# A recurrent attention and feed-forward kernel: heads of two pairs swapped over the array's rows from chunk 6 on

## The chip, the cores and the metric

One Trainium2 chip, one of its cores. The metric is device microseconds of one launch: the lower, the better. PE is the matrix engine, DVE the vector engine, ACT the scalar engine, POOL the general engine; SP only issues transfers here.

## What is computed

A linear recurrence over 768 time steps for 4 batches of 8 heads of size 48, then a feed-forward layer with a sigmoid gate:

```python
for t in range(S):
    cur = np.einsum('bhd,bhe->bhde', u[None] * kt, vt)
    y[:, :, t] = np.einsum('bhd,bhde->bhe', rt, state + cur)
    state = wt[:, :, :, None] * state + np.einsum('bhd,bhe->bhde', kt, vt)
...
h = x @ w_in                                    # x: 3072 tokens of 384, w_in: 384 x 2048
out = (h / (1 + np.exp(-1.702 * h))) @ w_out    # w_out: 2048 x 384
```

## The kernel before

**Chunks.** The 3072 tokens are 24 chunks of 128 (`chunk(t)`), six to a batch; the first chunk of a batch has no state to read, the last one makes none. Two heads are a pair, one in rows 0 to 63 of the array and one in rows 64 to 111 (`head(0)`, `head(1)`); there are four pairs. A chunk goes through these steps: two scans on DVE (lines 253, 259) give the products of decays; `kq` holds scaled keys and queries (274, 275); `ps_t` turns the keys round and ACT copies them to `kt` (309); ACT writes the eight diagonals of `am` (322); `ps_u` makes the new state (333), `sf`; `ps_s` are the scores, one bank of PSUM for each of the two row halves (351); DVE puts them into `am` where they count (354). Then the chunk's output is made of two parts on PE: `am` times the values (K is 128, two column halves) and the queries times the state (K is 64 or 48). ACT rounds the output into `x` (223) and DVE subtracts to get the remainder (224).

**Plain and crossed chunks.** Up to chunk 11 the two parts of the output go into one PSUM tile, `ps_y` (391, then 399): a head's rows and its output's partitions are the same half, so that the state part uses two of the array's four quarters. From chunk 12 on (`CROSS`) the two heads of pairs 2 and 3 are loaded with their rows swapped, in six transfers; the output is two tiles, `ps_c0` and `ps_c1` (363 for the state part, which comes first, then 369), one for each row half, and the state part uses all four quarters. Each of the two tiles is rounded and subtracted by itself. `x` of a crossed group has its blocks in another order on its lower rows.

**PSUM.** `ps_d`, `ps_t`, `ps_u`, `ps_s`, `ps_y` and `ps_c` share three buffers (`ps_a`, tag `psa`), taken in turn in the order in which the program asks for them: a tile waits until the third tile before it has been read for the last time.

**Feed-forward.** A group is four chunks. `ph` is x times a slice of w_in (two buffers), ACT makes `gh` and `gf` of it, DVE `gl`, and PE adds their products with w_out to `po`. Matmuls of 512 columns at float32r. The first 32 tasks use the whole array (lines 446 to 448 and 478 to 480), the later ones interleave the two row halves (504).

**Order.** Until task 32 the order on every engine is written out in the table `RAMP` (lN: a load of chunk N, aN: its next step, fN: a load of weights, wN: a step of their conversion, gN, hN, yN: the task N's three parts, xN: the moves that fill up x, kN: N matmuls that only keep PE busy); after that `PARTS` places the steps. Each engine works in its order, and a wait holds up all that is behind it on that engine. In `RAMP` the loads are issued by SP, later by POOL.

Of the kernel before, what the change touches and what calls it, by code (L numbers as in the profile page):

```python
# [8 lines left out]
F32 = mybir.dt.float32  # L9
# [50 lines left out]
RAMP = """  # L60
l0 l1 l0 a0 M l0 a0 a0 k20 a0 m0 m0 l1 a1 f1 l2 a0 f3 a1 l1 a0 a0 a1 k6 a0 l2 m1 a0 a1 a1 m1 a1 a0 a2 k5 a0 a1
a2 w1 k1 a1 a2 a1 k3 a2 l3 m2 f0 a2 a1 a3 a0 f0 k1 a2 k6 a1 l3 a3 l4 a2 a2 a3 a2 m3 k2 a3 a3 f6 a2 w0 a1 a4 k1
a3 w0 k6 a2 f2 l4 f8 l5 m3 a3 a3 a3 a3 a2 w1 f4 m2 k10 a3 f2 a3 a4 f8 w1 a4 w1 m4 k14 a4 a4 x3 l6 w0 w0 f11 a4
w2 a4 k3 a4 w2 a5 a4 g0 f4 h0 w2 g1 w2 g2 a5 f6 y0 w3 h1 g3 w4 w3 w4 h2 f10 f5 w3 m4 w3 y1 w4 f7 g4 y2 h3 a5 a4
y3 a5 w5 h4 w4 w6 l5 w5 m5 a5 w6 y4 g5 w5 g6 h5 f9 w6 w5 g7 w6 a5 w8 a4 a6 h6 w7 w8 w7 a6 a5 a5 a5 w8 a6 g8 a4
y5 h7 m6 f10 w8 w7 y6 h8 a5 w10 l7 g9 w7 a6 y7 h9 g10 a6 a7 m5 w10 y8 w9 w9 u a6 l6 a5 h10 a6 a5 w10 w9 a6 g11
w10 y9 g12 a7 h11 l8 w9 a7 h12 a7 w11 a7 l9 m7 a6 g13 w11 a6 g14 a7 w11 a8 w11 y10 a6 l7 h13 a6 a7 m6 a7 l8 a8
y11 m7 a8 g15 a7 l9 a7 a8 m8 a8 l10 a8 y12 h14 a7 a9 a7 a8 a9 a8 y13 a8 m8 y14 a8 a9 a9 m9 a9 l10 a9 a10 a8 m9
# [3 lines left out]
h26 y26 h27 y27 g28 g29 h28 g30 h29 a13 g31 a12 h30 y28 a12 a13 a13 m13 y29 a12 a12 h31 a13 a13 a13 m13 l14 l14  # L72
"""
WIDE = 512
CROSS = 12
WP = NF * DM // NL
SPLIT = range(FIRST, len(TASKS) - 1)
PHASE = 8
# [6 lines left out]
def rwkv_ffn_kernel(ctx: ExitStack, tc, wkr, vp, vrk, ub, w_in, w_out, masks, vt, uc, out):  # L85
# [58 lines left out]
    def load(t):  # L144

        assert t < 2 or loaded.get(t - 2, [None])[0] is None
        a, v = lands[t % 2], values[t % 3]
        loaded[t] = [a[0:R2], v]
        first, last = (TOP if t == 0 else 0), (R2 if t % (NT - 1) == 0 else P)
        rows = wkr.rearrange("t r w -> (t r) w")[t * R + first - TOP : t * R + last - TOP]  # L150
        n = NP * CW + 1
        if t < CROSS:
            for c0, c1 in ((0, n), (n, a.shape[1])) if t < 2 else ((0, a.shape[1]),):
                if c0:
                    yield
                behind_moves(queue[0].dma_start(a[first:last, c0:c1], rows[:, c0:c1]))
        else:
            w_, kr = slice(1, n), slice(n, a.shape[1])
            for cols, n_ in ((w_, 1), (kr, 2)):
                dst, src = (y[:, cols].rearrange("r (n q) -> r n q", n=n_) for y in (a, wkr[t]))  # L160
                one, two = (slice(h * dst.shape[2] // 2, (h + 1) * dst.shape[2] // 2) for h in range(2))
                queue[0].dma_start(dst[TOP:R2, :, one], src[:, :, one])
                for h in range(2):
                    rows = slice(TOP + h * D, TOP + (h + 1) * D)
                    queue[0].dma_start(dst[rows, :, two], src[(1 - h) * D : (2 - h) * D, :, two])
        yield
        assert t < 3 or t - 3 in weighed
        queue[0].dma_start(v[:, TOP:], vrk[t, :, 0:DM])
        if t >= WHOLE:
            rk = pools["late"].tile([P, 2 * DM], F32, tag="rk", name="rk_t")  # L170
            queue[0].dma_start(rk, vrk[t, :, DM:])
            loaded[t].append(rk)
        yield
# [3 lines left out]
    def fetch(i):  # L177

        s, which = divmod(i, 2)
        n = SL // NL  # L180
        st = staged[i] = wt.tile([P, n, 2 * WP // n], I32, tag=f"w{i}", name=f"raw{i}")
        src = (w_in, w_out)[which][s * n : (s + 1) * n].bitcast(I32)
        if which == 0:
            if s == 0:
                nc.sync.dma_start(st[TOP:], src[:, 0 : P - TOP].rearrange("n p w -> p n w"))
            else:
                rows = w_in.bitcast(I32).rearrange("s p w -> (s p) w")[s * n * P - TOP : (s + 1) * n * P - TOP]
                nc.sync.dma_start(st, rows.rearrange("(n p) w -> p n w", p=P))
            yield
            nc.sync.dma_start(st[0:TOP], src[:, P - TOP :].rearrange("n p w -> p n w"))  # L190
        else:
            nc.sync.dma_start(st, src.rearrange("n p w -> p n w"))
        yield

    def convert(i, pool, clamp):
# [44 lines left out]
    def chunk(t):  # L240
# [38 lines left out]
        if t < WHOLE:  # L279
            ps_d = ps_a.tile([P, NP, 2], F32, tag="psa", name="ps_d")  # L280
            for p in range(NP):
                T.matmul(ps_d[:, p], rk[:, p], u_heads[:, p], start=True, stop=True)
        yield
        if t < WHOLE:
            V.tensor_copy(s, ps_d.rearrange("p n h -> p (n h)"))
# [38 lines left out]
        def update():  # L324

            if final:
                return
            ps_u = ps_a.tile([R2, NP, D], F32, tag="psa", name="ps_u")
            for p in range(NP):

                for h in range(2):
                    c = TOP + name(p, h) * D
                    T.matmul(ps_u[head(h), p], kt[:, p, head(h)], v[:, c : c + D], start=True, stop=True)  # L333
            new = state[t] = states[t % 2]
            flat = ps_u.rearrange("r p d -> r (p d)")
# [19 lines left out]
        yield  # L355
        cs = slice(col * C, (col + 1) * C)
        if cross:
            ps = [ps_a.tile([R2, 2, C], F32, tag="psa", name=f"ps_c{r_}") for r_ in range(2)]
            each = [(p, r_, r_ ^ p // 2) for p in (0, 2, 1, 3) for r_ in range(2)]
            if sf is not None:  # L360
                for p, r_, o in each:
                    c = p * D
                    T.matmul(  # L363
                        ps[r_][head(o), p % 2], sf[head(r_), c + o * TOP : c + HB], qf[head(r_), p],
                        start=p in (0, 2), stop=False, skip_group_check=True,
                    )
            for p, r_, o in each:
                c = (2 * p + o) * D
                T.matmul(  # L369
                    ps[r_][head(o), p % 2], v[:, c + o * TOP : c + HB], am[r_][:, p],  # L370
                    start=sf is None and p in (0, 2), stop=p in (1, 3), skip_group_check=True,
                )
            weighed.add(t)
            yield
            if i not in xs:
                xs[i] = new_x(i)
            for b, y in enumerate(ps):
                split(*(xs[i][0:R2, n_, 2 * b : 2 * b + 2, cs] for n_ in range(2)), y)
# [30 lines left out]
        state.pop(t - 1, None)  # L409
        yield  # L410

    def fill_x(x, c0, c1, cross=False):

        for m in range(NM):
            for i, dst in enumerate((R2, 0)):
                j = TOP * (2 * m + i + 1)
                move = G.dma_start(  # L417
                    x[dst : dst + TOP, :, m ^ 2 * (cross and i == 0), c0:c1].bitcast(F32),
                    x[j : j + TOP, :, NM ^ 2 * (cross and j >= HB), c0:c1].bitcast(F32),
                )  # L420
                moves.append(move.ins.name)

# [14 lines left out]
    def first_product(j, task):  # L437
# [2 lines left out]
        plain = j < PLAIN  # L440
        ph = ps_h.tile([P, WIDE], F32, tag="ph", name="ph")[:, 0 : (c1 - c0) * C]
        o = by_twos(ph, plain)
        x = xs.get((i, 0), xs[i])
        for c in range(NM):
            h_, l_ = weight(0, f, c)
            T.matmul(o, h_, halves(x[:, 0, c, cs], plain), start=c == 0, stop=False)  # L446
# [66 lines left out]
    def first_rows(j, half):  # L513

        i, c0, c1, f = TASKS[j]
        cs = slice(c0 * C, c1 * C)
        if half == 0:
            parts[j] = ph_tile(c1 - c0)
        for n in range(3 * NM):
            c, term = divmod(n, 3)  # L520
            h_, l_ = weight(0, f, c)
            w, x = ((h_, 0), (h_, 1), (l_, 0))[term]
            end = n == 3 * NM - 1
            on_rows(
                half, ("h", j), parts[j], w, xs[i][:, x, c ^ 2 * (half and starts[i] >= CROSS), cs],
                half == 0 and n == 0, half == 1 and end, half == 0 and end,
            )
            yield
# [44 lines left out]
    def store(i, start, N, order=range(NM)):  # L573
# [9 lines left out]
            (A if late else queue[0]).dma_start(out[m, :, bass.ds(start, N)], ob)  # L583
        po.pop(i)
        xs.pop(i)
        xs.pop((i, 0), None)

    def new_x(i):

# [2 lines left out]
    with tc.manual_schedule():  # L592
# [17 lines left out]
        def do(token):  # L610
# [7 lines left out]
            elif kind == "x":  # L618
                group, col = where[i]
                if col == CHUNKS[group] - 1:  # L620
                    fill_x(xs[group], 0, (col + 1) * C, i >= CROSS)
            elif kind == "c":
                x = xs[i, 0] = new_x(i)
                for c in range(NM):
                    for rows, src in ((slice(0, HB), c), (slice(HB, P), c ^ 2)):
                        G.dma_start(x[rows, :, c].bitcast(F32), xs[i][rows, :, src].bitcast(F32))
            elif kind == "u":
                nc.sync.dma_start(u_sb, ub)
            elif kind == "M":
                A.dma_start(hm[TOP:R2], masks)  # L630
                for x in states + [v[:, 0:TOP] for v in values]:
                    G.memset(x, 0.0)
            elif kind == "k":
# [15 lines left out]
        def rest():  # L649
# [17 lines left out]
                        plan.setdefault(at_, []).append(token)  # L667
            for j in range(FIRST, len(TASKS) + LAG):
                for post in range(2):
                    if post and j == len(TASKS) - WHOLE:  # L670
                        yield f"c{len(CHUNKS) - 1}"
                    if post and j <= SPLIT[-1] + 1:
                        yield f"r{j}"
                        if j > SPLIT[0]:
# [137 lines left out]
```

## Time and profile before

| | us |
|---|---|
| median of 3 runs | 508.38 (506.61 to 509.78) |
| profiled execution | 508.68 |
| its span on the core | 506.7 |
| PE busy | 495.0 (98%) |
| ACT busy, DVE busy | 283.0, 285.3 (56% each) |

The table's busy times are over the whole span; the stages differ. Until about 47 us PE works mostly on matmuls that keep it busy while the first group's x is made, and from there to about 501 us it has feed-forward work in front of it all the time. DVE and ACT are nearly full until about 120 us and have room afterwards.

### The profile page before, as it was taken

To read this page: it belongs to the slowest core of one execution; us is meant where nothing else is said; L and a number is where in the kernel's file an instruction comes from. 1 tells how busy PE (TensorE), PEld (TensorE's weight loads), DVE (VectorE), ACT (ScalarE), POOL (GpSimd) and SP (SyncE) were. 2 spreads that over 40 slices of the span, in tenths; PEclk is the share of its full clock that TensorE was granted. 3 is DMA by queue.
4 is the path that set the end of the run, shared out by engine and by line. 5 is a ranking of instruction groups with operands and counts; after the bars stand their busy time and mean duration, and the time that the engine had idled before them with its cause. 6 is when DMAs were issued, how large, how long until landed. Compare 5 with 4: busy or idle time off the path is not lost.

```text
span 506.7 us, 11314 instructions
## 1 busy us (share of the span) xinstructions
PE 495.0 (98%) x4535; PEld 416.3 (82%) x4535; DVE 285.3 (56%) x443; ACT 283.0 (56%) x616; POOL 70.9 (14%) x144
## 2 busy tenths in 40 slices
PE   7999999999999999999999999999999999999995
PEld 4676788887888888888888889888888888888884
DVE  7898999998886213665565555556455421211110
ACT  4887989977865543366356365455465432422322
POOL 2002000000100200044103145104140002220000
PEclk9999999999999999999999999999999999999999
DMA  8996960125463300035112235112240001150001
GB/s 278 290 403 162 335 223 12 54 93 188 117 206 103 82 13 0 1 111 157 34 49 44 84 101 166 32 48 49 82 129 29 1 1 33 42 148 1 1 0 70
DMA packets 18171, 50.27 MB, mean 99 GB/s; under 512 B 3392, under 2 KB 7168, under 8 KB 18112
## 3 DMA queue, kind: packets, MB, share of 16 engines
q1 hardware_dynamic: 11376, 31.23, 19.0%
q0 software_dynamic: 6336, 17.72, 12.7%
q8 instruction: 38, 0.62, 0.5%
q10 hardware_dynamic: 400, 0.53, 0.3%
q14 instruction: 21, 0.17, 0.1%
HBM read 40.82 MB, written 4.72 MB: 90 GB/s over the span
## 4 chain that ended last, share of the span: by engine, by line
PE 85%; DMA 7%; DVE 3%; ACT 1%; SPq 1%; issue 0%; ACTq 0%; DVEq 0%
PE po L504 26%; PE ph L504 24%; DMA raw<-in_w_in 5%; PE po L478 4%; PE po L480 4%; PE po L479 4%; PE ph L446 4%; PE ph L448 4%; PE ph L447 4%; PE ps_s L351 3%; PE ps_c L369 2%; DMA v_t<-in_vrk 2%; PE ps_u L333 2%; PE ps_y L391 1%; PE ps_y L399 1%; PE ps_c L363 1%
## 5 line engine op out<-in xcount | busy, mean ns | idle before, releaser
L504 PE MATMUL ph<-x,pair 64*128 64x512 f32 x1134 | 185.7, 377 | 0.0
L464 DVE TENSOR_TENSOR gl<-gf,gh 128x512 fp32r<-128x512 f32 x96 | 66.3, 691 | 185.6 <-ACT gf L463 184.7
L504 PE MATMUL po<-gh,pair 64*128 64x512 f32 x768 | 157.8, 385 | 0.2 <-SPq L509 0.2
L504 PEld LDWEIGHTS ph<-x,pair 64*128 64x128 f32 x1134 | 143.6, 186 | 13.9
L463 ACT ACTIVATE gh<-ph 128x512 fp32r<-128x512 f32 x84 | 50.2, 597 | 159.1 <-PE ph L504 137.2
L504 PEld LDWEIGHTS po<-gh,pair 64*128 64x128 f32 x768 | 95.8, 187 | 10.5 <-issue 1.1
L504 PE MATMUL po<-gl,pair 64*128 64x512 f32 x384 | 99.3, 376 | 0.0
L322 ACT ACTIVATE am<-ident,s 128x128 f32<-128x128 f32 x192 | 58.7, 396 | 3.8 <-PE ps_y L391 2.3
L504 PEld LDWEIGHTS po<-gl,pair 64*128 64x128 f32 x384 | 50.1, 186 | 4.7
L417 POOL DMA_DIRECT2D x<-x x36 | 18.2, 512 | 247.7 <-DVE x L224 209.5
L463 ACT ACTIVATE gf<-ph 128x512 f32<-128x512 f32 x84 | 49.8, 593 | 0.0
L446 PE MATMUL ph<-x,pair 128*128 128x512 f32 x99 | 39.1, 395 | 1.2 <-DMA x<-x 0.6
L448 PE MATMUL ph<-x,pair 128*128 128x512 f32 x99 | 38.1, 385 | 0.2 <-DVE pair L214 0.2
L447 PE MATMUL ph<-x,pair 128*128 128x512 f32 x99 | 38.0, 384 | 0.0
L478 PE MATMUL po<-gh,pair 128*128 128x512 f32 x96 | 37.9, 394 | 0.0
L480 PE MATMUL po<-gl,pair 128*128 128x512 f32 x96 | 36.8, 384 | 0.0
L479 PE MATMUL po<-gh,pair 128*128 128x512 f32 x96 | 36.8, 383 | 0.0
L229 ACT ACTIVATE junk<-lp 112x1032 bf16<-112x1032 f32 x24 | 25.7, 1069 | 12.4 <-DVE lp L259 12.3
L253 DVE TENSOR_TENSOR_SCAN lp<-wkr_t,d1r 112x516 f32<-112x516 f32 x24 | 29.4, 1225 | 1.2 <-DMA wkr_t<-in_wkr 0.9
L259 DVE TENSOR_TENSOR_SCAN lp<-wkr_t,d1f 112x516 f32<-112x516 f32 x24 | 29.4, 1224 | 0.1
L354 DVE COPY_PREDICATED am<-after,ps_s 128x512 f32<-128x512 int32 x40 | 26.8, 724 | 1.9 <-PE ps_s L351 1.9
L229 ACT ACTIVATE junk<-kq 112x1024 bf16<-112x1024 f32 x24 | 25.4, 1058 | 1.4 <-DVE kq L275 1.3
(89 smaller groups left out, 640.4 us busy)
## 6 DMA issues: line engine op xcount, KB each, us to landing
wkr_t<-in_wkr SPq DMA_DIRECT2D x10, 770.5 KB, 5.4
raw<-in_w_out SPq DMA_DIRECT2D x6, 1024.0 KB, 11.2
raw<-in_w_in SPq DMA_DIRECT2D x5, 1024.0 KB, 11.8
rk_t<-in_vrk POOLq DMA_DIRECT2D x9, 384.0 KB, 3.6
out_t<-ob POOLq DMA_DIRECT2D x12, 256.0 KB, 2.7
v_t<-in_vrk SPq DMA_DIRECT2D x15, 192.0 KB, 4.9
rk_t<-in_vrk SPq DMA_DIRECT2D x7, 384.0 KB, 3.5
x<-x POOLq DMA_DIRECT2D x36, 64.0 KB, 2.6
```

The costliest lines, as they stand in the source:

```text
L229: A.activation(junk[:, 0 : x.shape[1]], x, AF.Square, accum_out=acc[0:R2, i : i + 1])
L253: V.tensor_tensor_scan(li.rearrange("r p c -> r (p c)")[:, ::-1], w1[:, ::-1], d1r.rearrange("r p c -> r (p c)")[:, ::-1], 0.0, op0=ALU.mu ...
L322: A.activation(x_[:, p], ident, AF.Copy, scale=s[:, j : j + 1])
L446: T.matmul(o, h_, halves(x[:, 0, c, cs], plain), start=c == 0, stop=False)
L447: T.matmul(o, h_, halves(x[:, 1, c, cs], plain), start=False, stop=False)
L448: T.matmul(o, l_, halves(x[:, 0, c, cs], plain), start=False, stop=c == NM - 1)
L463: A.activation(g, ph, AF.Gelu_apprx_sigmoid, scale=1.0 / W_SCALE)
L464: V.tensor_tensor(gl, gf, gh.bitcast(F32), op=ALU.subtract)
L478: T.matmul(o, h_, halves(gh, plain), start=first, stop=False, skip_group_check=True)
L479: T.matmul(o, l_, halves(gh, plain), start=False, stop=False, skip_group_check=True)
L480: T.matmul(o, h_, halves(gl, plain), start=False, stop=f == NF - 1, skip_group_check=True)
L504: mm = T.matmul(by_twos(out), w[rows], halves(x[rows]), start=start, stop=stop, skip_group_check=True)
```

## The change

From chunk 6 on (instead of 12) the heads of pairs 2 and 3 are swapped over the rows. The output of a crossed chunk now goes into one tile for pairs 0 and 1 and one for pairs 2 and 3, with every head on the partitions that it has in a plain chunk, so that x has one order for all groups: `fill_x` and `first_rows` lose their special cases, and the copy of the last group's x (`c`, six transfers by POOL) is gone. A crossed chunk's rows are loaded in nine transfers. A second, swapped copy of u (`um`) is loaded by POOL for chunks 6 and 7. In `RAMP` the load of chunk 6's rows (l6) stands behind most loads of weights, and loads of weights that stand behind x3 carry the wait for its moves themselves.

```diff
-a3 ... a4 a4 x3 l6 w0 w0 f11 a4
+a3 ... a4 a4 x3 w0 w0 f11 a4 w2
...
-... w5 m5 a5 w6 y4 g5 w5 g6 h5 f9 w6 w5 g7 w6 ...
+... w5 m5 a5 w6 y4 g5 w5 g6 h5 f9 l6 w6 w5 g7 w6 ...
...
-CROSS = 12
+CROSS = 6
...
+    um = cp.tile([R2, H], F32, name="um")
+    G.memset(um, 0.0)
+    u_crossed = um.rearrange("r (p h) -> r p h", h=2)
...
-            w_, kr = slice(1, n), slice(n, a.shape[1])
-            for cols, n_ in ((w_, 1), (kr, 2)):
-                ...
-                queue[0].dma_start(dst[TOP:R2, :, one], src[:, :, one])
+            for c0, n_ in ((1, n - 1), (n, NP * C), (n + NP * C, NP * C)):
+                one, two = (slice(c0 + h * n_ // 2, c0 + (h + 1) * n_ // 2) for h in range(2))
+                behind_moves(queue[0].dma_start(a[TOP:R2, one], wkr[t, :, one]))
                 for h in range(2):
                     rows = slice(TOP + h * D, TOP + (h + 1) * D)
-                    queue[0].dma_start(dst[rows, :, two], src[(1 - h) * D : (2 - h) * D, :, two])
+                    queue[0].dma_start(a[rows, two], wkr[t, (1 - h) * D : (2 - h) * D, two])
...
-            ps = [ps_a.tile([R2, 2, C], F32, tag="psa", name=f"ps_c{r_}") for r_ in range(2)]
+            ps = [ps_a.tile([R2, 2, C], F32, tag="psa", name=f"ps_c{b}") for b in range(2)]
...
-                        ps[r_][head(o), p % 2], sf[head(r_), c + o * TOP : c + HB], qf[head(r_), p],
+                        ps[p // 2][head(o), p % 2], sf[head(r_), c + o * TOP : c + HB], qf[head(r_), p],
...
-                    ps[r_][head(o), p % 2], v[:, c + o * TOP : c + HB], am[r_][:, p],
+                    ps[p // 2][head(o), p % 2], v[:, c + o * TOP : c + HB], am[r_][:, p],
...
-                    x[dst : dst + TOP, :, m ^ 2 * (cross and i == 0), c0:c1].bitcast(F32),
-                    x[j : j + TOP, :, NM ^ 2 * (cross and j >= HB), c0:c1].bitcast(F32),
+                    x[dst : dst + TOP, :, m, c0:c1].bitcast(F32),
+                    x[j : j + TOP, :, NM, c0:c1].bitcast(F32),
...
-                    if post and j == len(TASKS) - WHOLE:
-                        yield f"c{len(CHUNKS) - 1}"
```

PE, where the output of chunk 10 (`ps_y`, `ps_c`) is followed by the scores of chunk 11 (the second pair of `ps_s`); in brackets the semaphores that an instruction waits for. Before:

```order
L399 MATMUL ps_y<-kq,sf 64x128
L399 MATMUL ps_y<-kq,sf 48x128
L351 MATMUL ps_s_1763<-kq 128x128 [waits PE_49]
L351 MATMUL ps_s_1764<-kq 128x128 [waits PE_49]
L351 MATMUL ps_s_1763<-kq 128x128
L351 MATMUL ps_s_1764<-kq 128x128
```

Now:

```order
L370 MATMUL ps_c_1793<-am,v_t 48x128
L370 MATMUL ps_c_1794<-am,v_t 48x128
L370 MATMUL ps_c_1794<-am,v_t 64x128
L352 MATMUL ps_s_1832<-kq 128x128 [waits PE_49]
L352 MATMUL ps_s_1833<-kq 128x128 [waits DVE_49]
L352 MATMUL ps_s_1832<-kq 128x128
L352 MATMUL ps_s_1833<-kq 128x128
```

The third tile before `ps_s_1833` was one of chunk 10's own scores' tiles; it is now `ps_c_1793`, chunk 10's first output tile, and the wait for PE itself has become one for DVE. Between the two score tiles stands nothing else.

DVE in the same place, from chunk 10's `copy_predicated` to chunk 11's. Before:

```order
L354 COPY_PREDICATED am<-after,ps_s_1692 128x512
L259 SCALAR_TENSOR_TENSOR lp<-wkr_t,d1f 112x516
L269 TENSOR_TENSOR rk_t<-rk_t 128x384
L274 TENSOR_TENSOR kq<-wkr_t,lp 112x512
L275 SCALAR_TENSOR_TENSOR kq<-wkr_t,live,lp 112x512
L464 TENSOR_TENSOR gl<-gf,gh 128x512
L224 TENSOR_TENSOR x<-ps_y,x 112x4x128
L287 TENSOR_TENSOR rk_t<-rk_t,u_sb 128x384
L288 TENSOR_REDUCE s<-rk_t 128x8
L354 COPY_PREDICATED am<-after,ps_s_1763 128x512
```

Now:

```order
L355 COPY_PREDICATED am<-after,ps_s_1760 128x512
L260 SCALAR_TENSOR_TENSOR lp<-wkr_t,d1f 112x516
L270 TENSOR_TENSOR rk_t<-rk_t 128x384
L275 TENSOR_TENSOR kq<-wkr_t,lp 112x512
L276 SCALAR_TENSOR_TENSOR kq<-wkr_t,live,lp 112x512
L465 TENSOR_TENSOR gl<-gf,gh 128x512
L225 TENSOR_TENSOR x<-ps_c_1793,x 112x2x128
L225 TENSOR_TENSOR x<-ps_c_1794,x 112x2x128
L288 TENSOR_TENSOR rk_t<-rk_t,u_sb 128x384
L289 TENSOR_REDUCE s<-rk_t 128x8
L355 COPY_PREDICATED am<-after,ps_s_1832 128x512
```

One subtraction has become two in the same place; the one of `ps_c_1793` is the last reader of that tile. On ACT the two roundings of chunk 10 stand, as the one did, behind the eight diagonals of chunk 11.

SP, where the rows of chunk 9 stand ahead of the values of chunks 7 and 8. Before:

```order
L156 DMA wkr_t<-in_wkr 128x1541 x2
L168 DMA v_t<-in_vrk 128x384 x2
L171 DMA rk_t<-in_vrk 128x768
```

Now (the same, after the nine transfers of chunk 8):

```order
L163 DMA wkr_t<-in_wkr 96x258
L166 DMA wkr_t<-in_wkr 48x258 x2
L163 DMA wkr_t<-in_wkr 96x256
L166 DMA wkr_t<-in_wkr 48x256 x2
L163 DMA wkr_t<-in_wkr 96x256
L166 DMA wkr_t<-in_wkr 48x256 x2
L169 DMA v_t<-in_vrk 128x384 x2
L172 DMA rk_t<-in_vrk 128x768
```

SP has eight more transfers to issue ahead of the two chunks' values.

## Rows read from the trace of the kernel before

**Rows 1.** The page, part 2: PE's busy tenths in 40 slices.

```profile
PE   7999999999999999999999999999999999999995
```

**Rows 2.** Waits of PE, whole span: us in total, times, longest us.

```profile
PE ph L446 <- DMA x<-x: 0.6, 1, 0.6
...
PE ps_t L308 <- DVE kq L274: 0.5, 1, 0.5
```

**Rows 3.** Timeline of PE: chunks 9's and 10's outputs, 11's scores; start us, us.

```profile
145.08 1.09 PE L391 MATMUL ps_y<-am,v_t 128*64 128x128 f32 x16
...
156.96 1.09 PE L391 MATMUL ps_y<-am,v_t 128*64 128x128 f32 x16
157.98 1.08 PE L399 MATMUL ps_y<-kq,sf 64*64 64x128 f32 x16
159.00 1.16 PE L351 MATMUL ps_s<-kq 64*128 64x128 f32 x16
```

**Rows 4.** Timeline of PE, chunk 13 (crossed).

```profile
232.62 0.67 PE L363 MATMUL ps_c<-kq,sf 64*64 64x128 f32 x16
233.22 1.09 PE L369 MATMUL ps_c<-am,v_t 128*64 128x128 f32 x16
234.13 0.62 PE L333 MATMUL ps_u<-v_t,kt 128*48 128x48 f32 x16
```

**Rows 5.** Timeline of ACT, from chunk 10's diagonals to its rounding; idle time in brackets.

```profile
146.25 2.45 ACT L322 ACTIVATE am<-ident,s 128x128 f32<-128x128 f32 x8 [1.50 <-issue]
...
157.85 1.06 ACT L229 ACTIVATE junk<-lp 112x1032 bf16<-112x1032 f32 x1 [4.52 <-DVE lp L259]
...
159.87 2.44 ACT L322 ACTIVATE am<-ident,s 128x128 f32<-128x128 f32 x8
162.21 0.57 ACT L223 CAST x<-ps_y 112x512 fp32r<-112x512 f32 x1
```

**Rows 6.** Timeline of DVE, chunk 10.

```profile
153.37 0.69 DVE L464 TENSOR_TENSOR gl<-gf,gh 128x512 fp32r<-128x512 f32 x1 [1.18 <-ACT gf L463]
...
155.33 1.31 DVE L354 COPY_PREDICATED am<-after,ps_s 128x512 f32<-128x512 int32 x2
...
162.81 0.69 DVE L224 TENSOR_TENSOR x<-ps_y,x 112x512 fp32r<-112x512 f32 x1 [1.74 <-ACT x L223]
```

**Rows 7.** Lines 224 and 223: duration ns min/median/max, first and last start, forms.

```profile
L224 DVE TENSOR_TENSOR x<-ps_c,x x24: 413/420/427, 209.0 to 423.1; 112x256 fp32r<-112x256 f32 x24
...
L223 ACT CAST x<-ps_c x24: 372/375/378, 208.6 to 422.7; 112x256 fp32r<-112x256 f32 x24
```

**Rows 8.** Clock: timeline of PE at the start, windows at the end (PEclk after POOL).

```profile
2.82 6.07 PE L493 MATMUL idle<-d1r 112*128 112x512 bf16 x20 [2.82 <-POOL v_t L632]
...
9.96 1.46 PE L493 MATMUL idle<-d1r 112*128 112x512 bf16 x6
...
500.00:503.00 3.00, 1.21 (x6) 0.72 (x4) 0.00 (x0) 1.74 (x3) 0.00 (x0) 1.00 0.49 175
504.00:506.70 2.70, 0.00 (x0) 0.00 (x0) 0.00 (x0) 0.00 (x0) 0.00 (x0) 0.58 0.08 24
```

**Rows 9.** Weights' last early issue (SP), their landing, chunk 6's first scan (DVE).

```profile
51.57 0.37 SPq L192 DMA_DIRECT2D raw<-in_w_out  x1
...
DMA to landing us min/median/max: 7.7/11.1/18.4
...
76.81 1.23 DVE L253 TENSOR_TENSOR_SCAN lp<-wkr_t,d1r 112x516 f32<-112x516 f32 x1
```

**Rows 10.** Chunk 7's values: SP's issue, PE's use, transfers' us from issue to landing.

```profile
106.99 0.86 SPq L168 DMA_DIRECT2D v_t<-in_vrk  x2
...
113.42 0.62 PE L333 MATMUL ps_u<-v_t,kt 128*48 128x48 f32 x16
...
v_t<-in_vrk SPq DMA_DIRECT2D x15, 192.0 KB, 4.9
v_t<-in_vrk POOLq DMA_DIRECT2D x9, 192.0 KB, 2.8
```

More of the change, by code (lines that the diff above doesn't have):

```diff
@@ L62 @@
 a2 w1 k1 a1 a2 a1 k3 a2 l3 m2 f0 a2 a1 a3 a0 f0 k1 a2 k6 a1 l3 a3 l4 a2 a2 a3 a2 m3 k2 a3 a3 f6 a2 w0 a1 a4 k1
-a3 w0 k6 a2 f2 l4 f8 l5 m3 a3 a3 a3 a3 a2 w1 f4 m2 k10 a3 f2 a3 a4 f8 w1 a4 w1 m4 k14 a4 a4 x3 l6 w0 w0 f11 a4
-w2 a4 k3 a4 w2 a5 a4 g0 f4 h0 w2 g1 w2 g2 a5 f6 y0 w3 h1 g3 w4 w3 w4 h2 f10 f5 w3 m4 w3 y1 w4 f7 g4 y2 h3 a5 a4
-y3 a5 w5 h4 w4 w6 l5 w5 m5 a5 w6 y4 g5 w5 g6 h5 f9 w6 w5 g7 w6 a5 w8 a4 a6 h6 w7 w8 w7 a6 a5 a5 a5 w8 a6 g8 a4
+a3 w0 k6 a2 f2 l4 f8 l5 m3 a3 a3 a3 a3 a2 w1 f4 m2 k10 a3 f2 a3 a4 f8 w1 a4 w1 m4 k14 a4 a4 x3 w0 w0 f11 a4 w2
+a4 k3 a4 w2 a5 a4 g0 f4 h0 w2 g1 w2 g2 a5 f6 y0 w3 h1 g3 w4 w3 w4 h2 f10 f5 w3 m4 w3 y1 w4 f7 g4 y2 h3 a5 a4 y3
+a5 w5 h4 w4 w6 l5 w5 m5 a5 w6 y4 g5 w5 g6 h5 f9 l6 w6 w5 g7 w6 a5 w8 a4 a6 h6 w7 w8 w7 a6 a5 a5 a5 w8 a6 g8 a4
 y5 h7 m6 f10 w8 w7 y6 h8 a5 w10 l7 g9 w7 a6 y7 h9 g10 a6 a7 m5 w10 y8 w9 w9 u a6 l6 a5 h10 a6 a5 w10 w9 a6 g11
@@ L157, in load @@
         else:
-            w_, kr = slice(1, n), slice(n, a.shape[1])
-            for cols, n_ in ((w_, 1), (kr, 2)):
-                dst, src = (y[:, cols].rearrange("r (n q) -> r n q", n=n_) for y in (a, wkr[t]))
-                one, two = (slice(h * dst.shape[2] // 2, (h + 1) * dst.shape[2] // 2) for h in range(2))
-                queue[0].dma_start(dst[TOP:R2, :, one], src[:, :, one])
+            for c0, n_ in ((1, n - 1), (n, NP * C), (n + NP * C, NP * C)):
+                one, two = (slice(c0 + h * n_ // 2, c0 + (h + 1) * n_ // 2) for h in range(2))
+                behind_moves(queue[0].dma_start(a[TOP:R2, one], wkr[t, :, one]))
                 for h in range(2):
                     rows = slice(TOP + h * D, TOP + (h + 1) * D)
-                    queue[0].dma_start(dst[rows, :, two], src[(1 - h) * D : (2 - h) * D, :, two])
+                    queue[0].dma_start(a[rows, two], wkr[t, (1 - h) * D : (2 - h) * D, two])
         yield
@@ L184, in fetch @@
             if s == 0:
-                nc.sync.dma_start(st[TOP:], src[:, 0 : P - TOP].rearrange("n p w -> p n w"))
+                behind_moves(nc.sync.dma_start(st[TOP:], src[:, 0 : P - TOP].rearrange("n p w -> p n w")))
             else:
                 rows = w_in.bitcast(I32).rearrange("s p w -> (s p) w")[s * n * P - TOP : (s + 1) * n * P - TOP]
-                nc.sync.dma_start(st, rows.rearrange("(n p) w -> p n w", p=P))
+                behind_moves(nc.sync.dma_start(st, rows.rearrange("(n p) w -> p n w", p=P)))
             yield
-            nc.sync.dma_start(st[0:TOP], src[:, P - TOP :].rearrange("n p w -> p n w"))
+            behind_moves(nc.sync.dma_start(st[0:TOP], src[:, P - TOP :].rearrange("n p w -> p n w")))
         else:
-            nc.sync.dma_start(st, src.rearrange("n p w -> p n w"))
+            behind_moves(nc.sync.dma_start(st, src.rearrange("n p w -> p n w")))
         yield
@@ L281, in chunk @@
             for p in range(NP):
-                T.matmul(ps_d[:, p], rk[:, p], u_heads[:, p], start=True, stop=True)
+                T.matmul(ps_d[:, p], rk[:, p], (u_crossed if t >= CROSS else u_heads)[:, p], start=True, stop=True)
         yield
@@ L331, in update @@
                 for h in range(2):
-                    c = TOP + name(p, h) * D
-                    T.matmul(ps_u[head(h), p], kt[:, p, head(h)], v[:, c : c + D], start=True, stop=True)
+                    c = name(p, h) * D
+                    T.matmul(ps_u[head(h), p], kt[:, p, head(h)], v[:, TOP + c : TOP + c + D], start=True, stop=True)
             new = state[t] = states[t % 2]
@@ L410, in chunk, with fill_x @@
         yield
-    def fill_x(x, c0, c1, cross=False):
+    def fill_x(x, c0, c1):
         for m in range(NM):
@@ L442, in first_product @@
         o = by_twos(ph, plain)
-        x = xs.get((i, 0), xs[i])
+        x = xs[i]
         for c in range(NM):
@@ L524, in first_rows @@
             on_rows(
-                half, ("h", j), parts[j], w, xs[i][:, x, c ^ 2 * (half and starts[i] >= CROSS), cs],
+                half, ("h", j), parts[j], w, xs[i][:, x, c, cs],
                 half == 0 and n == 0, half == 1 and end, half == 0 and end,
@@ L585, in store @@
         xs.pop(i)
-        xs.pop((i, 0), None)
     def new_x(i):
@@ L620, in do @@
                 if col == CHUNKS[group] - 1:
[L621 to L626, printed above, removed]
+                    fill_x(xs[group], 0, (col + 1) * C)
             elif kind == "u":
@@ L630, in do @@
                 A.dma_start(hm[TOP:R2], masks)
+                G.dma_start(um[TOP:R2, 0 : H // 2], masks[:, 2 : 2 + H // 2])
+                for h in range(2):
+                    rows, others = (slice(g * D, (g + 1) * D) for g in (h, 1 - h))
+                    G.dma_start(um[TOP:R2][rows, H // 2 :], masks[others, 2 + H // 2 :])
                 for x in states + [v[:, 0:TOP] for v in values]:
```

## The prediction, made before the run

> **What bounds the kernel now.** I read the page's slices first: PE is at 9 tenths or more from the second slice to the last but one [rows 1]. The waits of PE say whether that means real saturation: after the first group's moves have landed and the feed-forward has begun (x<-x), the list holds little beyond one wait of 0.5 us for a transpose [rows 2]. So from about 47 us to the end PE is the bound: work taken off PE is worth its full time, and an idle stretch put on PE costs its full time, wherever it is. What comes before 47 us (chunks 0 to 3, their loads) is not touched, except for `um`. Third I read the timelines of PE, ACT and DVE around one chunk's output, since the change alters who waits for whom there.
>
> The sum is made against the profiled execution, 508.68 us; the median of the runs shown is 0.3 us lower, and I take that off at the end.
>
> **What PE saves.** In a plain chunk that has a state, the output takes from 156.96 to 159.00, 2.04 us, half of it the state part [rows 3]. In a crossed one it takes from 232.62 to 234.13, 1.51 us: the state part needs 0.60 us instead of 1.02, and the part with `am`, now second, 0.91 [rows 4]. That is 0.53 us, say 0.52, for each of the chunks 7 to 11. Chunk 6 has no state and keeps its eight matmuls: 0. Saved: 5 x 0.52 = 2.6 us.
>
> One rule speaks against this price. A plain chunk's state part writes one bank from both row halves, at different partitions, and its 16 instructions take 1.02 us, as do the 16 of the `am` part before it, which has no row halves [rows 3]; I see no sign that the halves take turns. The Trainium skill (TensorEngine Tiling (Array Packing), Gotcha 1: PSUM Pressure) says that different row tiles cannot access the same PSUM bank simultaneously. By it, the new tiles, each written from both row halves, would lose what crossing gives; the trace does not agree for halves that write different partitions. It is a rival below.
>
> **What PE waits for anew.** Three buffers serve all `psa` tiles in turn. A plain output takes one of them, a crossed one two. Of the chunks that change, only chunk 10 has its output followed directly by the next chunk's scores with nothing between, and there the second score tile now asks for the buffer of `ps_c0` of chunk 10. It is free when DVE has subtracted it, which needs ACT's rounding. PE is in order: the whole feed-forward stands behind that matmul.
>
> When does DVE do it? Before, the output of chunk 10 is finished at about 159, and the scores follow at 159.00 [rows 3], but ACT rounds it only at 162.21, behind the eight diagonals of chunk 11 [rows 5], and DVE subtracts at 162.81 [rows 6]. Nobody waited for that. Now PE does.
>
> - PE's lead when it reaches chunk 9's output: chunks 7 and 8, 1.04 us. It starts at 145.08 - 1.04 = 144.04; its `am` part is now second, from 144.64, and ends 1.09 later at 145.73, 0.44 ahead of the old 146.17 [rows 3].
> - ACT's diagonals of chunk 10 start when that has been read, at 146.25 before; they gain 0.44. Two roundings of chunk 9 instead of one cost 2 x 0.375 - 0.57 = 0.18 us [rows 5, 7]. So ACT is 0.26 us ahead, and so is what hangs on it: DVE's `gl`, which waits for ACT's `gf`, chunk 10's `copy_predicated` behind it [rows 6], the scan for which ACT waits 4.52 us, and chunk 11's diagonals [rows 5].
> - The rounding of `ps_c0` then starts at 162.21 - 0.26 = 161.95 and ends at 162.33; the subtraction takes 0.42 [rows 7] and ends near 162.8. PE goes on at about 162.85.
> - PE was ready: chunk 10's second `copy_predicated` ends at 155.33 + 1.31 - 0.26 = 156.38 [rows 6], the `am` part takes 0.91 [rows 4], so that PE stands before the scores' second tile at about 157.4.
>
> PE idles about **5.4 us**. The scores, which began at 159.00, now go on at 162.85: PE is 3.85 us late, in which the savings of chunks 7 to 10 are already used up. Chunk 11 gives back 0.52. Net **+3.3 us**, and no later cover: PE is the bound to the end, so nothing gives it back. The bounds of this term: ACT not ahead at all, +3.6; ACT ahead by all of PE's lead (1.56 us), +2.0.
>
> **The clock.** Granted clock at the end: the last matmuls stop at about 501.2, and in the last 2.70 us the mean is 0.58, which is the lower level (1.2 GHz instead of 2.4) from about 504.4 on, 3.2 us after PE went quiet [rows 8]. A stretch of 5.4 us can bring the same. The price: at the start, 20 matmuls of one form took 5.9 us until PE had the next kind of work, where later six take 1.46 [rows 8], some 0.22 each: about 1.6 us lost until the clock had risen. So the term lies between 0 and 1.6; I take the middle, +0.8, since the fall in the tail came after less idle time, but not surely within every such stretch. The Trainium skill (TensorE: Matmul & The Clock Gate, "Why this matters for your kernels") also warns of gaps between bursts of matmuls that put the clock back; the tail agrees.
>
> **Edits at nothing.** `um`: three small transfers, and memsets behind them, on POOL, which has nothing else to do there; the zeros are first read by chunk 0's output, in a stage where PE still fills its time [rows 1]. Extra roundings and subtractions of chunks 6 to 9: 0.2 us each of ACT and DVE, covered by PE's own work; if the cover were gone, 1 us in all. Chunk 6's load later, weights sooner: the rows' nine issues follow the weights' last at 51.57 and end near 56; even with the slowest landing of a weight, 18.4 us, they are there at 74.4, and the scan that needs them starts at 76.81 [rows 9]. If that cover were gone, DVE would lose what is missing, not PE at first. Weights that land sooner help ACT and DVE, not PE. Waits of the weights' loads for x3's moves: SP waited there before, at l6. The dropped copy of x by POOL: no wait of PE named it.
>
> **One load that may come late.** Chunk 9's rows are now nine issues instead of one ahead of chunk 7's values, 0.43 us each (two took 0.86): the issue moves from 106.99 to 110.4. A load of values takes 2.8 us on POOL's quieter queue and 4.9 as SP's median: it lands at 113.2 to 115.3, and PE wants it at 113.42 [rows 10]. So 0 to 1.9 us; I take 0, since little is queued ahead of it by then, and keep the rest for the range.
>
> **Sum.** 508.68 + 3.3 + 0.8 = 512.8; on the level of the median, **512.5 us**, 0.8% more.
>
> **Rivals.**
> - *The wait does not bite* (faster). If ACT rounded chunk 10 before PE got to the scores, only the saving is left: 508.4 - 2.6 = 505.8. It decides at 157.4: the subtraction must be done by then, 5 us earlier than its chain allows. For it: ACT has idle time ahead of 157.85. Against it: that idle time is a wait for DVE, and the diagonals and more stand between it and the rounding [rows 5].
> - *Row halves take turns in a bank.* The state part then costs 1.0 us again in chunks 7 to 11 (no saving, 2.1 us lost) and in the ten later crossed chunks (4.1 us): 511.7 + 6.2 = 517.9. This is the rule above. For it: the old crossed form kept each bank to one row half. Against it: rows 3.
> - *Chunk 7's values late as well:* up to 1.9 us on top, at the middle 513.5. For it: SP's issue time is certain. Against it: the wide old load was still moving when the values were issued, nine narrow ones will mostly be done.
>
> **Chances.** Forecast 0.78, wait does not bite 0.10, turns in a bank 0.04, values late 0.08. About 1% is what a measurement of this kernel can tell from no change; 1% is 503.3 and 513.5. Faster by over 1% would need twice the saving: 0.03. The forecast's own span is 510.1 (short stall, clock kept) to 513.6 (long stall, clock lost), to which the runs' own spread of some 1.5 us comes; a quarter of it, half of the late values and all of the turns lie above 513.5: 0.27. Within 1%: 0.70. The range leaves out the wait that does not bite and the turns: 508.5 to 516.
>
> **What would show it.** In the trace after: a wait of PE at `ps_s` for DVE's `x` at line 225, about 5 us, once, near 157 to 163, and no other new wait of PE; the outputs of chunks 7 to 11 at about 1.5 us; `ps_c` state parts of chunks 13 and later still at 0.6; a granted clock under 1 just after the stall, or not. Wrong, if that wait is missing or below 3 us, if the state parts take 1 us, or if PE waits for `v_t` at chunk 7's `ps_u`.

## The result, and the profile after

| | before | after |
|---|---|---|
| median | 507.55 us (506.61 to 509.78, 8 runs) | 513.26 us (510.93 to 514.83, 8 runs) |
| profiled execution | 508.68 | 512.76 |
| its span | 506.7 | 511.0 |

The ratio is 1.0105, with a 95% interval of 1.0078 to 1.0132: the changed kernel is 1% slower. The forecast was 512.5 us, 0.8% more, with the loss in one wait.

The page's slices of PE and of the granted clock show where to look, against [rows 1]:

```profile
PE   8998999999996999999999999999999999999995
...
PEclk9999999999997999999999999999999999999998
```

One slice, at 153 to 166 us, has dropped to 6 in PE, and the clock dropped in the same slice. The waits of PE, over the whole span (us in total, times, longest), hold one new entry, the first below, beside those that answer to [rows 2] (line numbers are those of the changed kernel, mostly one higher than before):

```profile
PE ps_s L352 <- DVE x L225: 4.9, 1, 4.9
...
PE ph L447 <- DMA x<-x: 0.8, 1, 0.8
...
PE ps_t L309 <- DVE kq L275: 0.5, 1, 0.5
```

The timeline of PE of the changed kernel, with chunk 7's output and the state update that follows it, chunk 10's output and chunk 11's scores, and chunk 13's output (it answers to [rows 3, 4]; start us, us):

```profile
120.60 0.67 PE L364 MATMUL ps_c<-kq,sf 64*64 64x128 f32 x16
121.20 1.09 PE L370 MATMUL ps_c<-am,v_t 128*64 128x128 f32 x16
122.11 0.62 PE L334 MATMUL ps_u<-v_t,kt 128*48 128x48 f32 x16
...
153.74 0.88 PE L364 MATMUL ps_c<-kq,sf 64*64 64x128 f32 x16
154.55 1.10 PE L370 MATMUL ps_c<-am,v_t 128*64 128x128 f32 x16
155.59 0.48 PE L352 MATMUL ps_s<-kq 64*128 64x128 f32 x2
160.95 2.08 PE L352 MATMUL ps_s<-kq 48*128 48x128 f32 x14 [4.88 <-DVE x L225]
162.96 0.79 PE L479 MATMUL po<-gh,pair 128*128 128x512 f32 x1
163.54 0.63 PE L480 MATMUL po<-gh,pair 128*128 128x512 f32 x1
...
166.94 0.38 PE L447 MATMUL ph<-x,pair 128*128 128x512 f32 x1
...
236.86 0.67 PE L364 MATMUL ps_c<-kq,sf 64*64 64x128 f32 x16
237.46 1.09 PE L370 MATMUL ps_c<-am,v_t 128*64 128x128 f32 x16
238.38 0.62 PE L334 MATMUL ps_u<-v_t,kt 128*48 128x48 f32 x16
```

Chunk 7's output now takes 122.11 - 120.60 = 1.51 us, and chunk 13's state part still 0.60. Chunk 10's output, though, takes 155.59 - 153.74 = 1.85 us: its second part (`am` times the values) starts at 154.55, 0.81 us behind the first, when DVE has just put chunk 10's scores into `am` (153.22 + 1.31 = 154.53).

```profile
153.22 1.31 DVE L355 COPY_PREDICATED am<-after,ps_s 128x512 f32<-128x512 int32 x2
```

PE begins chunk 11's scores at 155.59, stops after two matmuls and goes on at 160.95. What follows is slow: fourteen score matmuls last until the next start, 2.01 us, and nine products 166.94 - 162.96 = 3.98 us. From the first score to the last product it is 166.94 - 155.59 = 11.35 us. Without a wait the same work takes 3.14 (1.09 and 2.05 in the first experiment's rows below), so this place loses 8.2 us. The windows of the same kernel show why (from:to and length in us; busy us and number of instructions of PE, PE's weight loads, DVE, ACT and POOL; then PEclk, the mean granted clock; then DMA):

```profile
155.00:156.00 1.00, 1.00 (x14) 0.69 (x10) 1.00 (x3) 0.27 (x1) 0.00 (x0) 1.00 0.00 0
156.00:160.00 4.00, 0.07 (x1) 0.00 (x0) 2.04 (x4) 4.00 (x12) 0.00 (x0) 1.00 0.74 227
160.00:163.00 3.00, 2.05 (x15) 1.82 (x15) 2.12 (x5) 0.71 (x3) 0.00 (x0) 0.51 0.42 100
163.00:167.00 4.00, 4.00 (x11) 3.20 (x11) 1.00 (x2) 0.00 (x0) 0.00 (x0) 0.51 0.00 0
167.00:175.00 8.00, 8.00 (x41) 6.99 (x39) 0.69 (x1) 1.09 (x2) 0.00 (x0) 1.00 0.00 0
```

While PE stands idle the clock falls to the lower level (1.2 GHz), at about 160, and stays there until about 167, six microseconds into PE's work. The timelines of ACT and DVE of the changed kernel show what PE waits for [rows 5, 6]: ACT makes chunk 11's diagonals, then rounds chunk 10, and DVE subtracts.

```profile
157.75 2.44 ACT L323 ACTIVATE am<-ident,s 128x128 f32<-128x128 f32 x8
160.09 0.62 ACT L224 CAST x<-ps_c 112x256 fp32r<-112x256 f32 x2
```

```profile
160.47 0.76 DVE L225 TENSOR_TENSOR x<-ps_c,x 112x256 fp32r<-112x256 f32 x2 [1.89 <-ACT x L224]
```

### The profile page after: what moved, and what is told of

The parts are those of the page before. It is cut to its first block, busy times and chain, and to the rows that moved or that the text cites. A ratio compares the mean times of both kernels' runs of the same rounds, so it can differ in the third digit from the quotient of the medians.

```text
span 511.0 us, 11478 instructions
## 1 busy us (share of the span) xinstructions
PE 495.5 (97%) x4535; PEld 417.9 (82%) x4535; DVE 285.4 (56%) x449; ACT 283.5 (55%) x622; POOL 80.4 (16%) x169
## 4 chain that ended last, share of the span: by engine, by line
PE 89%; DMA 5%; DVE 2%; ACT 2%; issue 0%; POOL 0%; SPq 0%; ACTq 0%; DVEq 0%; POOLq 0%
PE po L505 25%; PE ph L505 24%; DMA raw<-in_w_in 5%; PE po L479 4%; PE po L481 4%; PE po L480 4%; PE ph L447 4%; PE ph L449 4%; PE ph L448 4%; PE ps_s L352 4%; PE ps_c L370 3%; PE idle L494 2%; PE ps_c L364 2%; PE ps_u L334 2%; PE ps_d L283 1%; PE ps_t L309 1%
## 5 line engine op out<-in xcount | busy, mean ns | idle before, releaser
L479 PE MATMUL po<-gh,pair 128*128 128x512 f32 x96 | 38.7, 403 | 0.0
L480 PE MATMUL po<-gh,pair 128*128 128x512 f32 x96 | 37.5, 391 | 0.0
L352 PE MATMUL ps_s<-kq 64*128 64x128 f32 (+1 forms) x320 | 23.7, 285 | 4.9 <-DVE x L225 4.9
```

The lines of the kernel that those rows point to most:

```text
L352: T.matmul(ps[h][:, p], kf[head(h), p], qf[head(h), p], start=True, stop=True)
L479: T.matmul(o, h_, halves(gh, plain), start=first, stop=False, skip_group_check=True)
L480: T.matmul(o, l_, halves(gh, plain), start=False, stop=False, skip_group_check=True)
```

## The experiments

The theory is that of the prediction with one size changed: five outputs save 0.53 us each, 2.65 in all (chunk 10's 1.85 us, seen above, would make it 4 x 0.53 + 0.19 = 2.3); one wait for a buffer of PSUM costs 4.9 us; the low clock behind it costs about 3. Rivals: the wait would only move if it were taken away; the slow matmuls behind it have another cause; the edits that I had put at nothing cost something.

Two tokens of `RAMP` matter here. The third `a11` behind `h20` is chunk 11's scores (the two before it are its diagonals and a step that issues nothing, as chunk 11 is the last of its batch), and the `a10` behind it is chunk 10's rounding and subtraction.

**1. Take the wait away (e1).**

```diff
-h20 a11 a11 a11 a10 y19 a12 a12 g21 g22 y20 a11 h21 y21
+h20 a11 a11 a10 y19 a12 a12 g21 g22 h21 y20 a11 a11 y21
```

On PE this puts the scores behind four blocks of products; on ACT and DVE it also puts task 21's middle part (`h21`) ahead of DVE's step that reads the scores.

> The changed kernel with chunk 11's scores moved, on PE alone, behind four blocks of feed-forward work that are ready (y19, g21, g22, y20; 7.8 us of matmuls), so that PE comes to them at about 163.7, after the subtraction that frees the buffer (161.2). Theory (the loss is this one wait and the clock behind it): the wait of 4.9 us at ps_s for DVE's x and the low clock after it are both gone; time 513.3 - 4.9 - 3.3 = 505.1. Rival (the wait only moves: PE then waits for chunk 11's copy_predicated or for gl, or for the next buffer): a new wait of 2 us or more near 165 to 172, time 508 or more. Rival (the swapped form itself costs, not the wait): still 511 or more.

Measured: 506.33 us median (503.94 to 509.47, 10 runs), ratio to the kernel before 0.9978 (0.9950 to 1.0005). PE's timeline in this kernel:

```profile
157.07 0.48 PE L479 MATMUL po<-gh,pair 128*128 128x512 f32 x1
...
159.12 0.38 PE L447 MATMUL ph<-x,pair 128*128 128x512 f32 x1
...
165.04 1.16 PE L352 MATMUL ps_s<-kq 64*128 64x128 f32 x16
166.13 0.48 PE L479 MATMUL po<-gh,pair 128*128 128x512 f32 x1
```

The scores run without a wait, 166.13 - 165.04 = 1.09 us, nine products take 159.12 - 157.07 = 2.05, and no other wait takes the old one's place. By the medians 6.9 of the expected 8.2 us came back, and the time is 1.2 above the theory's 505.1: the wait and what follows it are the loss, and the swapped form is not. Of the saving itself, the medians show only 0.9 us against the kernel before (507.25 on the same chip), with an interval that includes no change.

**2. Keep the wait, but keep PE busy in it (e3).**

```diff
-h20 a11 a11 a11 a10 y19
+h20 a11 a11 k22 a11 a10 y19
...
-        if 0 in po:
-            out, first = po[0][0], False
+        if po:
+            out, first = po[min(po)][0], False
```

> The changed kernel with 22 idle matmuls of 512 columns (22 x 0.216 = 4.75 us) put on PE between chunk 10's output and chunk 11's scores; they add zeros. Nothing waits less: DVE frees the buffer at the same moment. Theory (after the wait, the granted clock costs another 3.3 us, since PE stood idle): the clock stays at 1.00 through 155 to 170, the 14 scores' matmuls take about 1.1 us instead of 2.08, the products 0.216 us each; time 513.3 - 3.3 = 510.0. Rival (the scores and the products behind the wait are slow for another reason, such as reads or writes beside DVE): they stay slow, time 513.3, or more by what the extra matmuls last beyond the wait. Forecast's own term (0.8): 512.5.

Measured: 509.85 us (508.99 to 512.96, 6 runs), ratio 1.0069 (1.0041 to 1.0097). PE's timeline, and the windows as above:

```profile
155.34 4.92 PE L494 MATMUL po<-d1r 112*128 112x512 bf16 x22
160.19 1.67 PE L352 MATMUL ps_s<-kq 64*128 64x128 f32 x16
161.79 0.48 PE L479 MATMUL po<-gh,pair 128*128 128x512 f32 x1
...
163.84 0.38 PE L447 MATMUL ph<-x,pair 128*128 128x512 f32 x1
```

```profile
156.00:160.00 4.00, 4.00 (x20) 1.75 (x18) 1.80 (x3) 4.00 (x13) 0.00 (x0) 1.00 0.69 203
160.00:163.00 3.00, 2.97 (x24) 2.33 (x23) 2.74 (x6) 0.46 (x2) 0.00 (x0) 1.00 0.54 132
```

The 22 matmuls do no work that is wanted, yet the clock stays at 1.00, the nine products take 163.84 - 161.79 = 2.05 us again, and the place takes 163.84 - 155.34 = 8.50 us instead of 11.35. The difference, 2.85, is the clock's price, not 0.8; by the medians it is 3.4, by the two ratios 1.8 with intervals that overlap. So the rival is out: with the same steps of DVE and ACT beside them, the scores and products behind the wait are slow only when the clock is low.

**3. Shorten the wait on ACT (e5).**

```diff
-h20 a11 a11 a11 a10 y19
+h20 a10 a11 a11 a11 y19
```

> The changed kernel with chunk 10's two roundings on ACT ahead of chunk 11's eight diagonals (2.44 us) instead of behind them; DVE's and PE's orders stay. Theory (the length of the wait is set by what stands ahead of the rounding on ACT): the rounding starts at 157.75 instead of 160.09, the subtraction of ps_c0 ends near 158.9, and PE waits 2.9 us instead of 4.9. If the clock then stays up (it fell 4.0 us after PE went idle): 513.3 - 2.0 - 3.3 = 508.0; if it falls all the same: 511.3. Rival (the wait is for something else): still 4.9 us, 513.

Measured: 511.65 us (509.64 to 513.59, 5 runs), ratio 1.0080 (1.0036 to 1.0124). PE's timeline:

```profile
158.08 0.49 PE L352 MATMUL ps_s<-kq 64*128 64x128 f32 x2
161.47 1.37 PE L352 MATMUL ps_s<-kq 48*128 48x128 f32 x14 [2.90 <-DVE x L225]
162.77 0.79 PE L479 MATMUL po<-gh,pair 128*128 128x512 f32 x1
163.35 0.63 PE L480 MATMUL po<-gh,pair 128*128 128x512 f32 x1
...
166.24 0.38 PE L447 MATMUL ph<-x,pair 128*128 128x512 f32 x1
```

The wait is 2.90 us, as worked out: its length is set by what stands ahead of the rounding on ACT. The clock falls all the same, here when PE is already at work again: the products start 0.43 us apart at first, and the place takes 166.24 - 158.08 = 8.16 us, 5.0 more than without a wait. So the clock still costs some 2 us, and the time is near the one foretold for a clock that falls (511.3), not the 508.0 of one that stays up. In this execution (512.01 us) the clock was low a second time, from 49.6 to 53.0 us, behind a wait of 2.3 us for the first group's moves; the rows above lie outside that stretch.

**4. The rest of the change alone (e4, e7, e8, e10).** Crossed from chunk 12 as before, with the new form of the output, nine transfers, `um`, and the old table:

```diff
-CROSS = 6
+CROSS = 12
```

> The changed kernel with CROSS = 12 and the kernel before's table, so that chunks 6 to 11 are plain as before: what is left of the change is the new form of the crossed output (a tile for two pairs, each written from both row halves), the nine transfers for chunks 12 to 23, um, and no copy of x. Theory (row halves that write different partitions of a bank do not take turns; the other edits cost nothing): state parts of chunks 13 and later 0.6 us, no wait of 4.9 us, time 507.5 as before, within 0.5. Rival (turns in a bank): state parts 1.0 us, ten of them, 511.6. Rival (nine transfers come late): new waits of PE or DVE for wkr_t or v_t, 509 or more.

Measured: 510.22 us (507.26 to 512.81, 6 runs), ratio 1.0075 (1.0045 to 1.0105). I had expected 507.5, so the theory missed. Its profiled execution, at 507.26 the fastest of the six, has no new wait, and the state parts are as short as before, so this is not the rival with the banks; what the slower five did, no trace shows. Three runs took single edits out of it, or added one to the kernel before.

> The kernel of e4 (crossed from chunk 12, 510.2 us where 507.3 was expected) with um's three transfers issued behind the first group's moves (after 43 us) instead of at the start. Theory (um's transfers on POOL at 2.8 to 4.5 us, and the zeroing behind them, disturb the first stage, so that x3's moves land later in some executions): 507.5, as the kernel before. Rival (um costs nothing): 510.2 again.

Measured: 508.60 us (10 runs), ratio 1.0025 (1.0004 to 1.0045).

> The kernel of e4 with a crossed chunk's rows loaded in six transfers as before instead of nine, all else as in e4. Theory (the three more transfers per chunk, issued by POOL in chunks 12 to 23, make a load late in some executions): 507.5. Rival (the number of transfers costs nothing; the 3 us come from the first stage, before any crossed load): 510.2 again.

```diff
-for c0, n_ in ((1, n - 1), (n, NP * C), (n + NP * C, NP * C)):
-    ...
+w_, kr = slice(1, n), slice(n, a.shape[1])
+for cols, n_ in ((w_, 1), (kr, 2)):
+    ...
```

Measured: 508.81 us (10 runs), ratio 1.0025 (1.0009 to 1.0041). Each of the two edits, alone, leaves about 1 us against the kernel before, between its theory's 507.5 and its rival's 510.2. The two together would take back more than the fourth experiment lost, so these runs can't share its loss out.

> The kernel before with um alone added: its memset and its three transfers on POOL at the start; nobody reads it. Theory (um disturbs the first stage): slower than before by up to 3 us, 508.5 to 510.5, with a longer wait of PE for the first group's x near 46 us. Rival (um costs nothing): 507.3, as before.

Measured: 508.53 us (507.08 to 511.72, 10 runs), ratio 1.0024 (1.0001 to 1.0047).

The edit of e7 was this; e10 adds the lines with a minus to the kernel before, with um's memset:

```diff
 A.dma_start(hm[TOP:R2], masks)
-G.dma_start(um[TOP:R2, 0 : H // 2], masks[:, 2 : 2 + H // 2])
-...
 fill_x(xs[group], 0, (col + 1) * C)
+if i == 3:
+    G.dma_start(um[TOP:R2, 0 : H // 2], masks[:, 2 : 2 + H // 2])
+    ...
```

`um` alone costs about 1 us, with an interval that nearly touches nothing. The longer wait of PE near 46 us that I had foretold is not in the trace of this run: there PE does not wait for the first group's moves at all. The executions' mean granted clocks point to `um` all the same. Of the kernels in which PE does not idle at chunk 11, 14 of 42 executions had a mean of 0.995 or less with `um` at the start, 5 of 40 with `um` late, and 3 of 69 of the kernel before. The profile of the kernel with six transfers is one of them; PE at the start of the feed-forward, and the windows there:

```profile
47.71 0.77 PE L449 MATMUL ph<-x,pair 128*128 128x512 f32 x1 [2.91 <-DMA x<-x]
```

```profile
47.00:51.00 4.00, 3.29 (x8) 2.67 (x9) 1.62 (x2) 3.95 (x10) 0.00 (x0) 0.57 0.42 129
```

PE waited 2.91 us for the first group's moves, and the clock fell. That `um` makes such a wait likelier is not shown: in the traces PE waits longer than 1.5 us in two of the seven traces with `um` at the start and in two of the six others. How three transfers of 1.5, 0.8 and 0.8 KB, issued at 2.8 to 4.5 us, could act at 45 us was not seen either, and the rest of the 3 us of the fourth experiment stays open.

**5. Both moved, and chunk 6's load back in its old place (e9, e11, e13, e12).** The kernel of the first experiment with `um` late ran twice; then with l6 moved back, and as the changed kernel with nothing but `um` late.

> The kernel of e1 (506.3 us) with um's three transfers issued behind the first group's moves, as in e7. Theory (um disturbs the first stage): 505.0, the whole of the saving of 2.6 us. Rival (um costs nothing): 506.3 as e1.

Measured: 505.67 us (6 runs), ratio 0.9954 (0.9919 to 0.9989), between its theory's 505.0 and its rival's 506.3.

> The kernel of e9 (scores of chunk 11 behind the products, um late) in more runs, as the version that may beat both kernels. Theory (wait, clock and um are what kept the change from its saving): 2.6 us under the kernel before, with an interval that leaves 1 out. Rival (e9's 505.7 was chance): no different from the kernel before.

Measured: 505.50 us (503.11 to 507.94, 12 runs), ratio 0.9956 (0.9936 to 0.9976). So this version beats both kernels: it is 2.1 us under the kernel before (507.63 on the same chip), near the 2.3 that the outputs save, and 7.6 under the changed kernel with `um` late, which is next.

> The changed kernel with um's three transfers behind the first group's moves, all else as changed, the wait of 4.9 us too. Theory (the changed kernel's loss is 8.2 us of wait and low clock less 2.7 us saved, and up to 1 us of um's transfers at the start): 5 to 5.5 us above the kernel before, 512.5 to 513. Rival (um costs nothing): 5.7 above, as the changed kernel was. Rival (um is most of the loss): 510 or less.

Measured: 513.12 us (510.70 to 515.09, 6 runs), ratio 1.0096 (1.0068 to 1.0124). With the wait in place, `um` makes no difference that these runs can show.

```diff
-x3 w0 w0 f11 a4 w2 ... h5 f9 l6 w6
+x3 l6 w0 w0 f11 a4 w2 ... h5 f9 w6
```

> The kernel of e11 with chunk 6's load put back to where it was before, directly behind x3 and ahead of most weights, with its nine transfers. Theory (the place of that load costs and gives nothing, since its rows are wanted only at about 76 us): as e11, within 0.7 us. Rival (weights that are issued nine transfers later land late, and ACT, DVE or PE wait for them): 1 us or more above e11, with a wait of PE for pair or of ACT for raw between 50 and 75 us. Rival (chunk 6's rows come late in the new place): 1 us or more below e11.

Measured: 508.41 us (506.56 to 512.37, 12 runs), ratio 1.0031 (1.0010 to 1.0052): 2.9 us above the same kernel with the load late, on the same chip, so the rival holds and not the theory. SP's timeline, then ACT's, then a wait of PE, all of the kernel with the load early:

```profile
46.40 0.32 SPq L163 DMA_DIRECT2D wkr_t<-in_wkr  x1
...
50.50 0.42 SPq L193 DMA_DIRECT2D raw<-in_w_out  x1
```

```profile
58.69 1.10 ACT L204 ACTIVATE raw<-raw 128x1024 int32<-128x1024 uint32 x1 [4.09 <-DMA raw<-in_w_in]
```

```profile
PE ph L447 <- ACT gf L460: 2.8, 2, 2.4
```

Nine issues hold the weights back by 4.1 us; ACT waits 4.09 us for one, its later work is late, and PE waits 2.4 us for `gf`. In the kernel with the load late ACT has no such wait near 58 us.

## Why the prediction was right, and where a size was off

- **The wait:** right. Place, releaser and line are those foretold; 4.9 us instead of 5.4 (5.36 if counted from the start of the scores, 155.59). ACT reached the rounding at 160.09 instead of 161.95, mostly because the whole execution was earlier by then (PE at 155.59 instead of 157.4); DVE began the subtraction 0.38 us later, and PE went on at 160.95.
- **The saving:** right for four outputs, 1.51 us each as foretold. Chunk 10's takes 1.85 and saves 0.19, since PE stands there waiting for DVE; in all 2.3 us, not 2.6. In the changed kernel this costs nothing on top, as the wait behind chunk 10 takes in what was saved ahead of it, and the prediction had PE reach that wait only behind DVE's step. The row-halves rival is out: `ps_c`'s two tiles are each written from both halves, and the state part of chunk 13 still takes 0.60 us. The Trainium skill's sentence (TensorEngine Tiling (Array Packing), Gotcha 1: PSUM Pressure) does not hold here for halves that write different partitions of a bank.
- **The clock: the term that was mis-sized.** I had put it at 0.8 us, at most 1.6. It measured 3.0 us in the trace (the scores 2.01 - 14/16 x 1.09 = 1.06, the products 3.98 - 2.05 = 1.93) and 2.85 by the second experiment's trace. My upper end came from a stretch at the start in which the clock was low for less of PE's work. Here it fell within the wait, about 4 us after the last matmul, and PE then worked for 6 us at half speed, in which every matmul cost twice its time. What the term should have been: half of the low stretch that is filled with work, here 6.0 / 2 = 3.0, and in the third experiment, low from 162.3 to 165.7, 3.4 / 2 = 1.7. The Trainium skill (TensorE: Matmul & The Clock Gate, "Why this matters for your kernels") advises against idle gaps between bursts of matmuls beyond a length that it gives; the trace agrees for the gap of 4.9 us, the second experiment shows the gap's price apart from the wait's, and for shorter gaps the runs go both ways (last section).
- **Why 512.5 came out so near all the same:** in part by luck. I had the change at +4.1 us, and by the medians it is +5.7, as the clock took 2.2 us more than in the sum; but I started 0.8 us too high. Set against the profiled execution, 508.68 + 8.2 - 2.3 = 514.6, but the one after was 512.76. The execution of before from which I started had a wait in its first stage that the one after has not:

```profile
PE ps_u L333 <- DMA v_t<-in_vrk: 1.2, 1, 1.2
```

  Over 8 runs the kernel before has 507.55, 1.1 below that execution, where I had taken off 0.3. By the medians the loss is 5.7 us, by the place and the savings 8.2 - 2.3 = 5.9. One sum of the prediction is off: the lower end of the forecast's span (short stall, clock kept) is 508.4 + 2.0 = 510.4, not 510.1.
- **Edits at nothing:** the extra roundings and the dropped copy of x show in no wait of PE. Chunk 6's late load comes in time, but its issues took much longer than I had worked out, to 68 us instead of 56, as SP waited for other transfers between them; SP's first and last of them, and the scan that needs them, of the changed kernel [rows 9]:

```profile
52.33 0.34 SPq L163 DMA_DIRECT2D wkr_t<-in_wkr  x1
...
67.20 0.78 SPq L166 DMA_DIRECT2D wkr_t<-in_wkr  x2
```

```profile
75.09 1.22 DVE L254 TENSOR_TENSOR_SCAN lp<-wkr_t,d1r 112x516 f32<-112x516 f32 x1
```

  The scan had no wait ahead of it. I had priced the load's move at nothing against the kernel before; what I did not see is that nine transfers in the old place would have cost 2.9 us (the last experiment), which the move avoids. `um` I had at nothing; alone it measured 1.0 us, with an interval from nearly nothing to 2.4.
- **Chunk 7's values late:** no. The nine issues of chunk 9's rows were through at 106.9, since the wide old transfer had itself been held up on SP until 106.9 and the narrow ones start earlier; the values were issued at 107.01, as before [rows 10], and PE used them at 111.76 without a wait:

```profile
107.01 0.84 SPq L169 DMA_DIRECT2D v_t<-in_vrk  x2
```

```profile
111.76 0.62 PE L334 MATMUL ps_u<-v_t,kt 128*48 128x48 f32 x16
```

## What to carry to other kernels

Splitting one tile into two in a pool whose buffers go round shifts, for every tile behind it, which earlier tile it waits for; look for the place where the new owner is read late and nothing stands between on the in-order engine that is the bound. Where the granted clock falls behind an idle gap of the matrix engine, price the gap as itself plus half of the low-clock stretch that is filled with work. Fill the gap with work that is ready, as the order of four blocks did here (6.9 us back), rather than shorten it (1.6 us back for a wait 2.0 us shorter). Before costing a load at nothing, count its issues: nine of them held up all that stood behind them on the queue by 4.1 us.

## What the runs showed that I had not expected

The length of PE's wait for the first group's moves did not say whether the clock would fall behind it. In the profile of e11 it fell after 1.89 us (the matmuls start 0.42 us apart from 48.08 on):

```profile
47.21 0.47 PE L447 MATMUL ph<-x,pair 128*128 128x512 f32 x1 [1.89 <-DMA x<-x]
...
48.08 0.63 PE L447 MATMUL ph<-x,pair 128*128 128x512 f32 x1
48.50 0.63 PE L448 MATMUL ph<-x,pair 128*128 128x512 f32 x1
```

In that of e9, of the very same kernel, it stayed up after 2.47 us; PE's timeline, and the windows with PEclk 1.00:

```profile
48.96 0.47 PE L447 MATMUL ph<-x,pair 128*128 128x512 f32 x1 [2.47 <-DMA x<-x]
```

```profile
48.00:52.00 4.00, 3.04 (x13) 2.50 (x14) 1.01 (x1) 3.28 (x7) 0.50 (x1) 1.00 0.25 46
```

Behind the third experiment's wait (2.3 us) and the six-transfer kernel's (2.9 us) it fell, as in e11. What decides is open.
